# Chunked attention and gated feed-forward in one kernel: transposing transfers for q, k and P from tile 11 instead of tile 15, and batch 2's v loaded earlier

## The chip, the cores and the metric

One Trainium2 chip, one of its cores. The metric is the device time of one execution in microseconds (us): the median of 3 runs is 245.34 (245.0 to 245.46). A profiled execution of the same kernel took 244.74, of which the profile's span, from the first to the last instruction, is 242.7. The granted TensorE clock was 0.998 in it.

## What is computed

```python
# q, k, v: (4 batches, 8 heads, 768, 64); mem_k, mem_v: (4, 8, 8, 64)
for c in range(24):                       # chunks of 32 rows
    q_c = q[:, :, 32*c:32*c+32]
    k_full = [mem_k, k[16 rows left .. 8 rows right of the chunk]]    # v_full alike
    scores = q_c @ k_full.T / 8
    a = exp(scores - max); a = a / sum
    out[:, :, 32*c:32*c+32] = a @ v_full
x = out as 3072 tokens x 512
y = (relu(x @ w_gate) * (x @ w_val)) @ w_out       # 512 -> 1536 -> 512
```

The output is 3072 x 512 in float32.

## The kernel before

The 3072 tokens are 24 **tiles** of 128 rows, six to a batch: tile 11 is the last of batch 1, tiles 12 to 17 are batch 2. Attention works tile by tile, for all 8 heads at once. The feed-forward works on eight **blocks** of 2, 2, 2, 4, 4, 4, 4 and 2 tiles (block 3 is tiles 6 to 9, block 4 is tiles 10 to 13, block 5 is 14 to 17), so that its matmuls are 256 or 512 columns wide.

One tile's attention, in order:

- q and k are loaded by GpSimd's queue (load_qk, L250) into buffers qk_b, rows on partitions. They must be transposed to have the 64 elements of a head on partitions. Up to tile 14 TensorE does it (qk_t, L271: four transposes of 128x128 each for q and for k into PSUM, L275; then ScalarE or VectorE copies them to qT and kT, qk_copy L285). From tile LATE_QK = 15 on a **transposing transfer** does it (qk_transfer, L277, issued by SyncE at L283): q goes straight to qT, k to a buffer k_t (three of them), from which it is copied to kT.
- scores (L297): 32 small matmuls into s_ps, L309. A tile that isn't the last of its batch also needs k of the next tile.
- softmax: row_max and subtract on VectorE (L322, L329), exponent on ScalarE (L337), row_sum, reciprocal, normalise on VectorE (L341, L345, L352) into p_n (three buffers).
- P is transposed too: by TensorE up to tile 14 (p_t, L354: four transposes, L358, and a copy), from LATE_P = 15 on by a transposing transfer (p_transfer, L360, issued at L362) into pT.
- values (L368): 16 matmuls of P with v into xT_ps (L388), and a copy to the block's xT.

For batches 1 to 3, v lies in v_bd, two buffers used in turn: batch 2 has the one that batch 0 used, after it was set to zero (z0, L471 to L474), batch 3 the one of batch 1. A batch's v comes in two big transfers and two small ones (load_v_rows, L185), eight transfers put the memory's rows in (mem_rows, L168), and sixteen copies on ScalarE and VectorE duplicate rows within v_bd ("up", L194, L626).

The feed-forward of a block: 12 pairs of gate and value products (first, L407: g_ps, v_ps, four matmuls each), relu on ScalarE (L413), product on VectorE (gate, L419), then the output products (second, L432: 12 matmuls a tile), a copy and a store. g_ps, v_ps and out_ps share four PSUM banks.

**The order of the work** isn't written out. schedule() (L682) is a planner in Python that runs at build time: each op has engines with a cost, a list deps of ops that must be done (with a lag, if given), resources that it takes and gives, and a priority. The planner walks through a time of its own and hands each op to a free engine; the instructions are emitted in that order, and each engine then runs its own in order. The list deps is read by the planner alone: the semaphores on the chip follow from which tiles an instruction reads and writes, and from a rotation of eight semaphores for transfers of GpSimd's queue and eight for those of SyncE and ScalarE, so that at most eight are in flight. A transposing transfer costs ISSUE = 1.4 of SyncE in the plan and is taken as landed LAND = 4.5 (q, k) or LAND_P = 3.0 (P) later; work on TensorE that belongs to attention is planned a MARGIN of 1.0 after its inputs. GpSimd's transfers are not planned but listed: load() calls in a fixed order (L640 to L675); for batch 2 it is q, k up to k of tile 16 (late[5:21]), then the four of v and the eight memory rows, then q of tile 16 and on (late[21:33]).

Of the kernel before, what the change touches and what calls it, by code (L numbers as in the profile page):

```python
# [19 lines left out]
def kernel(  # L20
# [32 lines left out]
    BAND0 = 48  # L53
    UT = 3

    LATE_QK, LATE_P = 15, 15

    KEY_RUNS = ((0, CH, 0), (KW, 64, CH), (CH, KW, CTX))
    assert sum(BLOCKS) == NT and NMEM == 8 and D == 64 and H == 8
# [391 lines left out]
    def op(key, eng, fn, deps=(), prio=(0,), take=(), give=(), after=()):  # L451
        ops[key] = dict(eng=eng, fn=fn, deps=list(deps), prio=prio, take=list(take), give=list(give),
                        after=list(after))
# [7 lines left out]
    def psum16(n):  # L461
        return {"DVE": (0.07 + 0.52e-3 * n, 0.16 + 0.52e-3 * n), "ACT": psum(n)["ACT"]}
# [49 lines left out]
        return gone[-1:] if blk >= 2 else []  # L512


    ISSUE, LAND, SLACK, LAND_P = 1.4, 4.5, 1.0, 3.0

    def pace_t(a):
        return [("s", a - 6)]

    for a in range(NT):  # L520
        b, t = divmod(a, TPB)
        last = t == TPB - 1
        for i in (1, 0):
            if b == 0:
                if t % 2 == 0:
                    for j in range(2):
                        op(("t", a + j, i), {"PE": 0.3}, lambda e, a=a, i=i, j=j: pair_t(a // 2, i, j),
                           [("pl", a // 2, i), "ib", ("new", b)], (1, a - i, -2 + j), ["aps"])
                        op(("tc", a + j, i), psum16(HP * 128) if t else {("ACT", "DVE")[j]: psum16(HP * 128)[("ACT", "DVE")[j]]}, lambda e, a=a, i=i, j=j: pair_copy(a // 2, i, j, engine[e]),
                           [("t", a + j, i)], (1, a - i, -2 + j), (), ["aps"])  # L530
                continue
            if a >= LATE_QK:
                op(("t", a, i), {"SP": ISSUE}, lambda e, a=a, i=i: qk_transfer(a, i),
                   [(("qk", a, i), SLACK), ("new", b)],
                   (1, a - i, 0), ["kt"] if i else [], [("qk", LAND)], pace_t(a))
                if i:
                    op(("tc", a, i), {"DVE": (0.2, 0.29), "ACT": (0.52, 0.62)}, lambda e, a=a, i=i: qk_copy(a, i, engine[e]),
                       [(("t", a, i), LAND)], (1, a - i, 0), (), ["kt"])
                continue
            op(("t", a, i), {"PE": 0.24}, lambda e, a=a, i=i: qk_t(a, i), [("qk", a, i), "ib", ("new", b)],  # L540
               (1, a - i, 0), ["aps"], ["qk"], pace(max(a - i, 0)))
            op(("tc", a, i), psum16(HP * 128), lambda e, a=a, i=i: qk_copy(a, i, engine[e]), [("t", a, i)],
               (1, a - i, 0), (), ["aps"])
# [38 lines left out]
    for rank, (blk, m) in enumerate(seq):  # L582
        n = BLOCKS[blk]
# [34 lines left out]
    for b in range(1, B):  # L618
        for n in range(2 * HP):
            hp, par = divmod(n, 2)  # L620
            for m in range(TPB // UT):
# [3 lines left out]
                   lambda e, b=b, par=par, i0=i0, i1=i1: upper(b, par, i0, i1, engine[e]),  # L625
# [13 lines left out]
    late = [(a, i) for a in range(TPB, NT) for i in (1, 0)]  # L639
# [22 lines left out]
    for b in range(1, B):  # L662
        deps = ([("z0", hp, c0) for hp in range(HP) for c0 in range(0, NCH, 8)] if b > 1 else [("z1", hp) for hp in range(HP)]) + ([("v", TPB * (b - NSET + 1) - 1)] if b > NSET else [])
        if b == 1:
            for n in range(2 * HP):
                op(("mr", b, n), {"SP": 0.72}, lambda e, n=n: mem_rows(nc.sync, 1, n),
                   deps + [(("vm", 0), 0.2), (("vm", 1), 0.2)], (0,))
        for par in range(2):
            load_v_op(b, par, deps)
        if b > 1:  # L670
            for n in range(2 * HP):
                load(("mr", b, n), 192, 0.22, lambda b=b, n=n: mem_rows(nc.gpsimd, b, n),
                     deps + [(("vm", 0), 0.2), (("vm", 1), 0.2)])
        for a, i in late[5 if b == 1 else 9 + 12 * (b - 1):21 + 12 * (b - 1)]:
            load_qk_op(a, i)  # L675

    WARM = 18.0
# [4 lines left out]
    def schedule():  # L682
        done, started, times = {}, set(), [0.7]
        free = {e: 0.7 for e in ("PE", "ACT", "DVE", "SP", "POOL")}
        queue_end, flying, gives = 0.0, [], [(WARM + 0.15, "fps")]
# [28 lines left out]
        while len(started) < len(ops) + len(loads):  # L714
            t = heapq.heappop(times)
            while times and times[0] <= t + 1e-9:
                heapq.heappop(times)
            for g in [g for g in gives if g[0] <= t + 1e-9]:
                gives.remove(g)
                room[g[1]] += 1  # L720
            flying = [f for f in flying if f > t]
            moved = True
            while moved:
                moved = False
                for e in ("POOL", "PE", "ACT", "DVE", "SP"):
                    if free[e] > t + 1e-9:
                        continue
                    if e == "POOL":
                        if n_load == len(loads):
                            continue  # L730
                        o = loads[n_load]
                        if len(flying) >= 8 or not ready(o, t):
                            continue
                        n_load += 1
                        key = o["key"]
                        if o["n"]:
                            end = t + 0.62 + 0.27e-3 * o["n"]
                            queue_end = max(queue_end, end + 0.8) + o["work"]
                            flying.append(queue_end + 1.0)
                            done[key] = queue_end + (1.2 if n_load < 8 else 4.5 if key[:2] == ("vl", 1) else 2.4 if n_load < 45 else 6.0 if key[0] == "vl" else 4.0)  # L740
                        else:
                            end = done[key] = t + max(o["work"], 0.6)
                        fn = o["fn"]
                    else:
                        o = None
                        soon = False
                        for _, key in todo[e]:
                            late_pe = e == "PE" and t > 36.0 and ops[key]["prio"][0] == 1
                            if ready(ops[key], t, MARGIN if late_pe else 0.0):
                                o = None if soon and key[0] in ("up", "z0") else ops[key]  # L750
                                break
                            soon = soon or ready(ops[key], t + 0.3)
                        if o is None:
                            if e == "PE" and 1.3 < t < WARM:
                                order.append((t, lambda: idle_product(256)))
                                free[e] = t + (0.213 if t < 9.0 else 0.11)
                                heapq.heappush(times, free[e])
                            elif e == "PE" and t <= 1.3:
                                heapq.heappush(times, 1.31)
                            continue  # L760
                        for x in o["eng"]:
                            todo[x].remove((o["prio"], key))
                        d = o["eng"][e]
                        d, lat = d if isinstance(d, tuple) else (d, d)
                        d *= (1.8 if e == "PE" and t < 8.0 and key[0] in ("t", "p", "sh", "f") else 1.0)
                        end = t + d
                        done[key] = end + 0.25 if e == "PE" else t + lat + 0.08

                        if queue_end > t:
                            queue_end += 1.1 if e == "SP" and key[0] in ("t", "pc") else 0.7 if key[0] == "oc" else 0.0  # L770
                        fn = lambda o=o, e=e: o["fn"](e)
                        for g in o["give"]:
                            g, lag = g if isinstance(g, tuple) else (g, 0.0)
                            gives.append((done[key] + lag, g))
                            heapq.heappush(times, done[key] + lag)
                    for r in o["take"]:
                        room[r] -= 1
                    started.add(key)
                    for k in users.get(key, ()):
                        missing[k] -= 1  # L780
                        if not missing[k]:
                            offer(k)
                    order.append((t, fn))
                    free[e] = end
                    for x in (end, done[key], done[key] + 0.2, done[key] + 1.5, done[key] + MARGIN):
                        heapq.heappush(times, x)
                    moved = True
            assert times, [k for k in ops if k not in started][:20]
        return order

    for _, fn in schedule():
        fn()
# [30 lines left out]
```

## Time and profile before

| what | value |
|---|---|
| median of 3 runs | 245.34 us |
| profiled execution | 244.74 us, span 242.7 us |
| TensorE matmul busy | 235.8 us, 97% of the span |
| VectorE, ScalarE, GpSimd busy | 61%, 56%, 32% |
| q, k transposes on TensorE at L275 | 72 |
| P transposes on TensorE at L358 | 60 |
| transposing transfers: k_t, qT, pT | 9, 9, 9 |
| loads of q and of k at L254 | 18 and 18, 128 KB each, 7.0 and 7.2 us from issue to landing in the median |
| first transfer of batch 2's v | issued at 67.46 us |

Times of instructions are counted from the span's start. The page's first part gives busy time for each engine, the second the span in 40 slices of 6.07 us with a digit of busy tenths each; "DMA" there is the mean busy share of the core's 16 DMA engines. "PE" is TensorE's matmuls, "PEld" its weight loads, DVE VectorE, ACT ScalarE, POOL GpSimd, SP SyncE. A matmul's duration in the group rows is its latency; matmuls overlap, so what one costs on a busy TensorE is read from the distance to the next start, or from the chain of work that ended last. For transfers, the trace also has the times at which their semaphores rise, 16 steps for each; "landing" below is the last of these.

### The profile page before, as it was taken

The numbers are of one execution on the slowest core, as the hardware profiler recorded it, in microseconds if no ns is written. First come the engines' busy times: TensorE is split into PE (matmuls) and PEld (weight loads), VectorE is DVE, ScalarE is ACT, GpSimd is POOL, SyncE is SP. The second block draws the span as 40 slices with busy tenths as digits, with TensorE's granted clock in tenths as the row PEclk, the third lists the DMA queues.
The fourth block names the chain that finished last, engine by engine and source line by source line (L and its number), as shares of the span: only waits on it lengthen the run. The fifth ranks groups of instructions, "written<-read, shape, count | busy, mean of one in ns | idle before, by whom it ended". The sixth has DMA issues, their size and how long they took to land.

```text
span 242.7 us, 6546 instructions
## 1 busy us (share of the span) xinstructions
PE 235.8 (97%) x2706; PEld 140.8 (58%) x2706; DVE 147.9 (61%) x296; ACT 136.0 (56%) x288; POOL 77.9 (32%) x102
## 2 busy tenths in 40 slices
PE   7898999999999999999999999999999999999994
PEld 5587887884589545554544545554445444445873
DVE  6674876988877458977549999894431043410430
ACT  7477777767885499665756674453332233312432
POOL 8975689235984396037430000000000000000000
PEclk9999999999999999999999999999999999999999
DMA  6999999999999999999990142651001210012102
GB/s 72 172 179 203 201 164 172 193 131 134 191 195 154 80 168 136 120 124 153 116 218 7 36 53 48 131 133 24 0 0 46 86 43 0 3 43 86 43 3 86
DMA packets 96413, 25.17 MB, mean 104 GB/s; under 512 B 87424, under 2 KB 93312, under 8 KB 96384
## 3 DMA queue, kind: packets, MB, share of 16 engines
q0 software_dynamic: 76128, 14.65, 83.5%
q1 hardware_dynamic: 16656, 3.82, 15.0%
q10 hardware_dynamic: 3600, 6.29, 8.1%
q8 instruction: 21, 0.34, 0.7%
q14 instruction: 8, 0.07, 0.1%
HBM read 28.55 MB, written 6.29 MB: 144 GB/s over the span
## 4 chain that ended last, share of the span: by engine, by line
PE 88%; ACT 4%; DMA 2%; POOL 2%; DVE 2%; issue 1%; ACTq 0%; POOLq 0%
PE v_ps L407 26%; PE g_ps L407 25%; PE out_ps L432 22%; PE xT_ps L388 3%; DMA v_n<-in_v_dram 2%; PE s_ps L309 2%; PE idle_ps L141 2%; PE vs_ps L215 2%; PE xT_ps L381 2%; PE pT_ps L358 2%; ACT v_bd L79 1%; PE qk_ps L275 1%; PE qk_ps L236 1%; POOL qk_p L227 1%; ACT o_sb L79 1%
## 5 line engine op out<-in xcount | busy, mean ns | idle before, releaser
L419 DVE TENSOR_TENSOR gvT<-v_ps,g_relu 128x256 f16<-128x256 f32 (+1 forms) x96 | 52.9, 554 | 58.2 <-PE v_ps L407 43.2
L407 PE MATMUL v_ps<-xT,w_val_sb 128*128 128x256 f16 (+1 forms) x384 | 78.2, 326 | 0.1
L407 PE MATMUL g_ps<-xT,w_gate_sb 128*128 128x256 f16 (+1 forms) x384 | 78.2, 326 | 0.0
L413 ACT ACTIVATE g_relu<-g_ps 128x256 f16<-128x256 f32 (+1 forms) x96 | 47.0, 491 | 47.6 <-PE g_ps L407 45.9
L432 PE MATMUL out_ps<-w_out_sb,gvT 128*128 128x512 f16 (+2 forms) x300 | 65.3, 371 | 0.0
L407 PEld LDWEIGHTS <-w_gate_sb 128*128 128x128 f16 x384 | 36.3, 98 | 23.1
L407 PEld LDWEIGHTS <-w_val_sb 128*128 128x128 f16 x384 | 36.0, 98 | 22.3 <-issue 0.5
L432 PEld LDWEIGHTS <-gvT 128*128 128x128 f16 x300 | 27.9, 98 | 29.9
L79 ACT COPY o_sb<-out_ps 128x512 f32<-128x512 f32 (+2 forms) x25 | 14.2, 567 | 31.8 <-PE out_ps L432 25.6
L337 ACT ACTIVATE p_exp<-dif 128x256 f16<-128x256 f32 (+2 forms) x72 | 19.6, 340 | 4.4 <-DVE dif L329 3.5
L322 DVE TENSOR_REDUCE mx<-s_ps 128x8 f32<-128x512 f32 x24 | 16.5, 688 | 5.6 <-PE s_ps L309 5.4
L341 DVE TENSOR_REDUCE sm<-p_exp 128x8 f32<-128x512 f16 x24 | 16.4, 683 | 4.4 <-ACT p_exp L337 4.1
L254 POOL DMA_DIRECT2D qk_b<-in_q_dram x18 | 16.4, 912 | 7.4 <-DMA v_bd<-in_v_dram 5.5
L254 POOL DMA_DIRECT2D qk_b<-in_k_dram x18 | 16.2, 903 | 5.5 <-DMA w_out_sb<-in_moe_w_out_dram 4.4
L79 ACT COPY v_bd<-v_bd 24x768 f16<-24x768 f16 (+1 forms) x20 | 15.6, 818 | 2.2 <-ACT o_sb L79 1.2
L352 DVE TENSOR_TENSOR p_n<-p_exp,rinv 128x512 f16<-128x512 f16 x24 | 16.5, 687 | 0.4
L329 DVE TENSOR_TENSOR dif<-s_ps,mx 128x512 f32<-128x512 f32 x24 | 16.4, 682 | 0.2
L185 POOL DMA_DIRECT2D v_bd<-in_v_dram x12 | 10.9, 920 | 12.5 <-PE v_ps L407 11.8
L168 POOL DMA_DIRECT2D v_bd<-vmem x16 | 10.5, 661 | 12.5 <-DMA v_bd<-in_v_dram 10.5
L79 ACT CAST xT<-xT_ps 128x512 f16<-128x512 f32 x17 | 9.9, 583 | 6.2 <-PE xT_ps L388 4.8
L141 PE MATMUL idle_ps<-idle 128*128 128x256 bf16 x69 | 11.5, 319 | 1.1 <-DVE warm L475 1.1
L388 PEld LDWEIGHTS <-v_bd 128*128 128x128 f16 x288 | 9.7, 96 | 3.2 <-issue 0.2
(57 smaller groups left out, 179.5 us busy)
## 6 DMA issues: line engine op xcount, KB each, us to landing
out_dram<-o_sb ACTq DMA_DIRECT2D x23, 256.0 KB
qk_b<-in_k_dram POOLq DMA_DIRECT2D x18, 128.0 KB, 7.2
qk_b<-in_q_dram POOLq DMA_DIRECT2D x18, 128.0 KB, 7.0
v_bd<-in_v_dram POOLq DMA_DIRECT2D x6, 384.0 KB, 11.5
w_out_sb<-in_moe_w_out_dram POOLq DMA_DIRECT2D x2, 768.0 KB, 10.5
qk_p<-in_k_dram POOLq DMA_DIRECT2D x3, 256.0 KB, 5.7
qk_p<-in_q_dram POOLq DMA_DIRECT2D x3, 256.0 KB, 6.6
v_n<-in_v_dram POOLq DMA_DIRECT2D x6, 128.0 KB, 6.5
```

The source lines that it names most:

```text
L79: nc.scalar.copy(o, i)
L254: nc.gpsimd.dma_start(qk_b[a, i], bass.AP(tensor=x.tensor, offset=x[b, 0, 128 * t, 0].offset, ap=[[D, 128], [S * D, H], [1, D]]))
L322: nc.vector.reduce_max(SM[a, "mx"], s4, axis=AX.X)
L329: nc.vector.tensor_tensor(out=SM[a, "dif"].rearrange("p (m r) a s -> p r m a s", r=2), in0=S_ps.pop(a).rearrange("p r (m a) s -> p r m a s ...
L337: nc.scalar.activation(p[:, :, :, s0:s0 + k1 - k0], dif[:, :, :, k0:k1], ACT.Exp, scale=SCALE)
L341: nc.vector.reduce_sum(SM[a, "sm"], SM[a, "p"], axis=AX.X)
L352: nc.vector.tensor_tensor(out=P_n[a], in0=SM.pop((a, "p")), in1=rinv_b, op=ALU.mult)
L388: nc.tensor.matmul(ps[:, hp, r], lhsT=v_bd[b % NSET][:, hp, 4 * t + g, :], rhs=x[:, hp, r], start=True, stop=True)
L407: nc.tensor.matmul(ps, lhsT=w[:, f, 128 * m:128 * m + 128], rhs=xTs[blk][:, f, :], start=(f == 0), stop=(f == NFC - 1))
L413: nc.scalar.activation(st["r", m], st.pop((0, m)), ACT.Relu)
L419: nc.vector.tensor_tensor(out=st["gv"][:, m, :], in0=st.pop((1, m)), in1=st.pop(("r", m)), op=ALU.mult)
L432: nc.tensor.matmul(st["o", t, c], lhsT=st["gv"][:, m, 128 * t:128 * t + 128], rhs=w_out_sb[:, m, c[0]:c[1]], start=(m == 0), stop=(m == ND ...
```

## The change

```diff
-    LATE_QK, LATE_P = 15, 15
+    LATE_QK, LATE_P = 11, 11
...
-    ISSUE, LAND, SLACK, LAND_P = 1.4, 4.5, 1.0, 3.0
+    ISSUE, LAND, SLACK, LAND_P = 1.5, 5.0, 1.0, 4.5
...
             if a >= LATE_QK:
                 op(("t", a, i), {"SP": ISSUE}, lambda e, a=a, i=i: qk_transfer(a, i),
-                   [(("qk", a, i), SLACK), ("new", b)],
+                   [(("qk", a, i), SLACK), ("new", b)] + [("vl", 2, n) for n in range(2) if 10 <= a < 15],
                    (1, a - i, 0), ["kt"] if i else [], [("qk", LAND)], pace_t(a))
...
-        for a, i in late[5 if b == 1 else 9 + 12 * (b - 1):21 + 12 * (b - 1)]:
+        for a, i in late[(5, 14, 33)[b - 1]:(14, 33, 36)[b - 1]]:
             load_qk_op(a, i)
...
                         if queue_end > t:
-                            queue_end += 1.1 if e == "SP" and key[0] in ("t", "pc") else 0.7 if key[0] == "oc" else 0.0
+                            queue_end += 1.5 if e == "SP" and key[0] in ("t", "pc") else 0.7 if key[0] == "oc" else 0.0
```

q, k and P of tiles 11 to 14 go by transposing transfers instead of TensorE. In the plan, the q and k transfers of tiles 11 to 14 wait for the two big transfers of batch 2's v ("vl"). In GpSimd's list the four transfers of that v and its eight memory rows stand before k of tile 13 instead of after k of tile 16: seven loads move behind them. The plan takes a transposing transfer as longer (ISSUE, LAND, LAND_P, and 1.5 instead of 1.1 added to its estimate of the busy DMA queue). pace(), which in the plan keeps a tile's transposes on TensorE back until the feed-forward has come to a certain point, then holds for tiles up to 10 instead of 14; a transfer is only placed after the scores of the tile six before it (pace_t).

## Prediction

> **What bounds the kernel now.** First the busy shares, then the span in slices:
>
> ```profile
> PE 235.8 (97%) x2706; PEld 140.8 (58%) x2706; DVE 147.9 (61%) x296; ACT 136.0 (56%) x288; POOL 77.9 (32%) x102
> PE   7898999999999999999999999999999999999994
> DMA  6999999999999999999990142651001210012102
> ```
>
> TensorE is full in every slice but the first four and the last, so time is saved only by taking work from it, and lost where it waits. The DMA engines are full until slice 21 (127 us) and nearly idle later. Next the chain of work that ended last:
>
> ```profile
> 86.69 0.45 PE qk_ps L275 x8
> 87.13 0.86 PE v_ps L407 x4
> ...
> 92.66 0.45 PE qk_ps L275 x8
> ...
> 234.36 4.55 PE out_ps L432 x24
> 238.94 0.49 ACT o_sb L79
> ```
>
> From 80 us on it is TensorE alone, and the transposes stand in it: eight at L275 move the next product by 0.45 us. The timeline of TensorE gives the other steps: 0.86 for four matmuls of 512 columns, 0.65 for three of L432, 0.22 for four P transposes (96.74 to 96.96), about 0.34 for a tile's scores, 0.40 for its values. I added these along the program's order from the start of block 3 (85.66): for the kernel before, the last output products come out at 234.39; the chain has 234.36. So there is no hidden wait in this stretch, and the same sum over the changed order gives due times.
>
> **What the change removes.** By the two programs' orders, TensorE loses 32 transposes at L275 (q, k of four tiles) and 16 at L358. 32 x 0.45/8 = 1.78 us and 16 x 0.22/4 = 0.88 us: **2.66 us** of the chain. Until 85.66 TensorE's order is the same in both. The sum over the changed order ends at 231.73 instead of 234.39 if nothing waits. On VectorE and ScalarE eight copies out of PSUM go (q and P, 0.42 or 0.58 each), and four of k read k_t instead (0.28 or 0.62); those engines are 61% and 56% busy, beside TensorE: I count nothing.
>
> The groups with their shapes show another number:
>
> ```profile
> L358 PE MATMUL pT_ps<-band,p_n 128*128 128x128 f16 x60 | 5.8, 220 | 0.2 <-DVE qT L81 0.2
> L275 PE MATMUL qk_ps<-ident_b,qk_b 128*128 128x128 bf16 x72 | 5.8, 220 | 0.0
> ```
>
> 220 ns is one transpose from its start to its end, but they overlap; only the step of 56 ns is worth anything on a full engine. The Trainium skill, page "TensorE: Matmul & The Clock Gate", Part 4: PE-mode transpose, gives about 275 ns for a transpose in a kernel's context; as an estimate 48 of these would be 13.2 us. No row of the chain agrees.
>
> **What it adds.** Twelve transposing transfers of 128 KB, all in the full stretch. In the plan those of q and k wait for batch 2's v; in the program no semaphore of v stands ahead of them. Each waits for its own load, for its place in the rotation of eight, and k for a free k_t. So k of tile 11 is issued when it has landed, at 63.5, behind nothing on SyncE. The issues before:
>
> ```profile
> 60.81 0.88 POOL L254 DMA_DIRECT2D qk_b<-in_k_dram  x1
> ...
> 67.46 1.33 POOL L185 DMA_DIRECT2D v_bd<-in_v_dram  x1 [0.52 <-DVE p_n L352]
> ```
> ```profile
> 71.98 1.31 SPq L283 DMA_TRANSPOSE k_t<-qk_b  x1
> ...
> 98.82 2.69 SPq L283 DMA_TRANSPOSE qT<-qk_b  x1
> 101.72 1.75 SPq L283 DMA_TRANSPOSE k_t<-qk_b  x1
> 103.56 1.28 SPq L283 DMA_TRANSPOSE qT<-qk_b  x1
> ...
> 136.57 1.19 SPq L362 DMA_TRANSPOSE pT<-p_n  x1
> ```
>
> Before, too, the first (k of tile 15) left as soon as its load was there (71.96). By the landing semaphores, these transfers took 8.6, 8.6, 7.7, 6.3 and 2.4 us; the longest took 11.5 (issued at 73.50, beside v) and 10.4 (91.32), the shortest of the full stretch 4.0 (107.23).
>
> **Step 1, v of batch 2.** Its first transfer leaves at 60.8 instead of 67.46 (the seventh load earlier; v_bd is cleared by 56). Before, both halves had landed 15.3 us after the first issue, at 82.75, with three transposing transfers between; now four lie between: 60.8 + 15.3 + some 1.4 = 77.5 (each such transfer takes at most 242.7 x 15.0% / 27 = 1.35 us of all 16 engines, by the queue row "q1 hardware_dynamic: 16656, 3.82, 15.0%"). This matters as the copies within v_bd now stand earlier on both engines: after 33 relus on ScalarE stands one that waits for the second half, reached at about 78.5. Of TensorE's work only the last product of block 2's first output tile is behind it; adding copy, relu and gate (0.83, 0.42, 0.42), TensorE waits only if v lands after about 81. Cost 0 at 77.5.
>
> **Step 2, q and k of tile 13 on.** These loads now follow v: before, the next load left 1.5 us after v (84.26) and landed after 4.35; so k of tile 13 lands at about 83.5, and with the latencies before (7 to 10 us) k13 is transposed at about 90.5 and k14 at 96.5; scores of tiles 12 and 13 are due at 98.9 and 102.3, and the copies to kT stand on ScalarE at about 98 and 99. Two to seven us spare. k15 must wait for the k_t of tile 12, whose copy stands behind the fourth relu of block 3 (93.7): it lands at about 101.5, and the relu behind its copy can bear 104. Cost 0.
>
> **Step 3, P of tile 11.** The tightest. Scores of tile 11 are due at 92.29; in VectorE's new order normalise stands behind the gate of block 3's sixth pair, which TensorE ends at 97.0; gate, reciprocal and normalise (0.69, 0.12, 0.69) give 98.6, the issue 98.7. SyncE is free by then: q of tile 15 left at about 95. Values of tile 11 are due at 106.07: **7.4 us** for the transfer, where TensorE's transpose and copy needed less than 2. Bounds from rows: 2.4 (alone, at 136.57) and 10.4 or 11.5 (deepest queue), so a wait of 0 to 3.0 or 4.1. I take 8.1, the middle of 8.6, 7.7 and 6.3 leaned to the later rows' upper end, since loads are still running (19 behind v instead of 12) and two or three transposing transfers are outstanding: **0.7 us** of waiting. Behind it in TensorE's order stands everything, so this is lost; but the deadlines that follow move along.
>
> **Step 4, the next ones.** k16 and q16, k17, q17 queue behind P of tile 11 on SyncE, 1.3 us apart. By the same sums P12 has 8.4 us, P13 7.7 and P14 about 7, and k16 some 9 before its copy holds back relus and scores. The 0.7 waited in step 3 is added to each of P12's and P13's, whose softmax comes before the wait or beside it. From 107 the third batch's v is in the queue; beside it transfers took 7.0 (108.79) and 6.5 (115.85), what P14 has. So 0 more, with 2 as the other end (10.4 at P13). After 127 transfers take 2.4 to 4 and have 7: nothing.
>
> **Sum.** -2.66 + 0.7 = -1.96. Profiled 244.74 - 1.96 = 242.8 (span 240.7); the median of the runs stands 0.6 above the profiled execution: 245.34 - 1.96 = **243.4**.
>
> **Rivals.** *All hidden*: the transfers take 7.4 or less at step 3, as at 103.56 (6.3): 242.7. For it: the 7.4 us given; TensorE's order leaves more to the rest. The Trainium skill, "Advanced Engine Details and Errata", X-Bar Transpose, says that on trn2 transposing DMAs are as fast as regular ones. The page's regular loads of 128 KB take 7.0 and 7.2 in the median here, which would lead to this case; the rows of 8.6 speak against it, that of 2.4 is from an idle stretch.
>
> *P arrives late* (the other side): values wait for pT. Each us over 7.4 costs one; from 10.1 the gain is gone. At the 10.4 of 91.32, with the 0.5 us more for tile 12 or 13, whose softmax doesn't move with the wait: 245.34 - 2.66 + 3.0 + 0.5 = 246.2. For it: the deepest queue, twelve more transfers in a full stretch. Against: only one row of the 98 to 107 stretch is that long, when five were outstanding.
>
> *The hold isn't one*: k11 to q12 run beside v as said, and v comes no earlier than before, 82.75. Then ScalarE's copy blocks relu and gate: 82.75 - 81 = 1.7 us, 244.4 with step 3 in its place. Against: 15.3 us from issue held with other transfers between.
>
> *Transposes cost their duration*: 48 x 0.22 = 10.6 off, 234.8. The steps in the chain deny it.
>
> **How the numbers follow.** Forecast 0.5 (243.4, own range 242.9 to 244.3), all hidden 0.25, P late 0.15, no earlier v 0.09, full duration 0.01. A change of 0.2% (0.5 us) is about what a measurement tells from none. Faster takes nearly all of the first two (0.73), half of the case without an earlier v, and the last: 0.78. The rest of that case and the nearest part of P late give 0.10 within; the remainder, 0.12, is slower. The range goes from 242.4, the full 2.66 with 0.3 for the rows' rounding and the runs' spread, to 245.4, which takes in half of P late; outside stay the rest of it, the last rival and little else, under 0.2.
>
> **What would show it.** After: 40 and 44 transposes at L275 and L358; the last output products at 231.7 plus the waits; idle time of TensorE before L388 "<-DMA pT<-p_n", about 0.7 in total; k_t issued at 63.5, ahead of v's landing at 77.5; no wait before L407 or L432 at 78 to 86. Wrong it would be if TensorE waits before L309 for qT or kT, if a gate or relu stands behind a v_bd or kT copy for over 1 us, or if transfers of P take over 10 us at 98.

## The result and the profile after

The changed kernel takes **257.74 us** (median of 6, 255.09 to 262.63), the kernel before 244.80 in the same batch: a ratio of 1.0474 (1.0408 to 1.054). 243.4 was predicted: by the medians it lost 12.9 us instead of gaining 2.0. The ratio is of the four shorter of the six runs; the other two, both at 262, are left out of it, and as the profiled execution (262.63, span 260.9) is one of these, kinds and places of the waits are read from it and differences from the runs' times.

First part and slices of the profile after, as shown of before:

```profile
PE 239.1 (92%) x2658; PEld 139.5 (53%) x2658; DVE 147.8 (57%) x291; ACT 135.3 (52%) x285; POOL 77.6 (30%) x102
PE   7998999999989899759993699999999999999994
PEclk9999999999999999977998899999999999999999
DMA  7999999999998999999999991151001320002102
```

A slice is 6.52 us here. TensorE is no longer full in several of the slices 12 to 23 (72 to 150 us), its granted clock dips in 18, 19, 22 and 23, and the DMA engines are nearly full until slice 24 (157 us) instead of 21 (127 us). TensorE's waits, from its timeline (start, time, engine, line, operation; in brackets the idle time before and what ended it):

```profile
78.72 0.60 PE L407 MATMUL g_ps<-xT,w_gate_sb 128*128 128x256 f16 x4 [1.74 <-ACT g_relu L413]
...
86.46 2.98 PE L432 MATMUL out_ps<-w_out_sb,gvT 128*128 128x512 f16 x13 [1.09 <-DVE gvT L419]
...
107.55 0.30 PE L309 MATMUL s_ps<-kT,qT 64*32 64x64 bf16 x26 [1.41 <-ACT kT L79]
...
112.25 1.02 PE L407 MATMUL g_ps<-xT,w_gate_sb 128*128 128x512 f16 x4 [1.71 <-ACT g_relu L413]
115.13 0.59 PE L388 MATMUL xT_ps<-pT,v_bd 128*128 128x32 f16 x16 [1.86 <-DMA pT<-p_n]
...
142.25 0.59 PE L388 MATMUL xT_ps<-pT,v_bd 128*128 128x32 f16 x16 [4.54 <-DMA pT<-p_n]
...
148.98 0.55 PE L388 MATMUL xT_ps<-pT,v_bd 128*128 128x32 f16 x16 [2.40 <-DMA pT<-p_n]
```

The first two stand behind ScalarE's copies within v_bd: one starts at 77.43, when the first half of batch 2's v has landed (77.41), one at 84.70, when the second has (84.68). The third and the fourth (a relu that stands behind a copy on ScalarE) wait for k of tiles 14 and 15, which landed at 106.86 and 111.07; the last three are values waiting for P. From the chain of work that ended last:

```profile
63.86 20.82 DMA v_bd<-in_v_dram
...
85.56 0.39 ACT g_relu L413
...
85.97 0.44 DVE gvT L419
...
86.46 2.98 PE out_ps L432 x13
...
103.66 11.43 DMA pT<-p_n
115.09 0.04 issue
115.13 0.59 PE xT_ps L388 x16
...
125.11 7.95 DMA pT<-p_n
133.06 0.05 issue
133.32 15.62 DMA pT<-p_n
148.94 0.04 issue
148.98 0.55 PE xT_ps L388 x16
```

Before, this chain was TensorE alone from 80 us on; now a transfer of 20.82, one of 11.43 and one of 15.62 stand in it. With one more wait of 0.20 before L388 the waits add to 14.95. Span against span the loss is 260.9 - 242.7 = 18.2; with 2.66 saved, 5.9 are left beyond the waits. Most of that is the clock after the waits. The windows of 2 us (length, TensorE's busy time, then PEld, DVE, ACT, POOL, the granted clock, DMA share, GB/s):

```profile
112.00:114.00 2.00, 1.02 (x4) 0.39 (x4) 1.76 (x3) 0.69 (x2) 0.87 (x1) 1.00 2.72 152
114.00:116.00 2.00, 0.87 (x49) 0.74 (x48) 1.68 (x4) 1.54 (x5) 0.00 (x0) 0.58 1.46 80
116.00:118.00 2.00, 2.00 (x17) 0.73 (x6) 0.81 (x3) 0.96 (x2) 1.45 (x2) 0.50 1.68 153
118.00:120.00 2.00, 2.00 (x6) 0.76 (x5) 1.88 (x3) 0.31 (x1) 0.37 (x1) 0.50 1.67 157
120.00:122.00 2.00, 2.00 (x39) 0.67 (x36) 0.60 (x1) 0.98 (x4) 1.63 (x2) 0.71 1.85 154
...
140.00:142.00 2.00, 0.00 (x0) 0.00 (x0) 0.61 (x1) 0.00 (x0) 0.00 (x0) 0.91 1.45 65
142.00:144.00 2.00, 1.75 (x20) 0.92 (x20) 0.00 (x0) 1.12 (x4) 0.00 (x0) 0.50 1.31 119
144.00:146.00 2.00, 2.00 (x9) 0.77 (x8) 1.34 (x3) 0.41 (x3) 0.00 (x0) 0.74 1.59 111
```

The clock is 0.50 behind the waits at 112 to 115 and behind that of 4.54; products of 512 columns that step by 0.86 elsewhere step by 1.70 to 1.82 there. What is missing from a clock of 1.00 in these windows adds up to 5.1 us (2 us times each shortfall), the most that it can have cost; some of it fell on idle time. So the clock is most of the 5.9 and not all; the rest is not traced. The Trainium skill, "TensorE: Matmul & The Clock Gate", Why this matters for your kernels, warns of gaps over about 3 us between bursts of matmuls; the trace agrees for the wait of 4.54, while the first halving stands behind two shorter waits, 1.71 and 1.86, with 1.0 us of work between.

The queues, from GpSimd's and SyncE's timelines:

```profile
62.05 3.67 POOL L185 DMA_DIRECT2D v_bd<-in_v_dram  x4
```
```profile
64.50 1.31 SPq L283 DMA_TRANSPOSE k_t<-qk_b  x1
65.92 1.57 SPq L283 DMA_TRANSPOSE qT<-qk_b  x1
67.58 2.50 SPq L283 DMA_TRANSPOSE k_t<-qk_b  x1
70.27 1.21 SPq L283 DMA_TRANSPOSE qT<-qk_b  x1
```

So v did leave earlier, and the four transfers the plan had placed behind its landing left while it was in flight. By the landing semaphores that v came at 84.68 (77.5 was predicted, 82.75 it was before), the four took 9.3 to 15.6 us, and batch 3's v, issued at 116.55 instead of 107.01, took 30.0 us instead of 11.5, beside transposing transfers of 7.1 to 15.6. A late v also holds up the loads behind it, which GpSimd issues in their listed order:

```profile
77.69 0.63 POOL L168 DMA_DIRECT2D v_bd<-vmem  x1 [8.50 <-DMA v_bd<-in_v_dram]
...
84.96 1.26 POOL L168 DMA_DIRECT2D v_bd<-vmem  x2 [5.32 <-DMA v_bd<-in_v_dram]
86.21 1.06 POOL L254 DMA_DIRECT2D qk_b<-in_k_dram  x1
```

It stood idle for 8.50 and 5.32 us until v's halves had landed, so k of tile 13, the load at 86.21, left late.

### The profile page after: what moved, and what is told of

Read it like the earlier page. It is cut to its first block, busy times and chain, and to the rows that moved or that the text cites. A ratio compares the mean times of both kernels' runs of the same rounds, so it can differ in the third digit from the quotient of the medians.

```text
span 260.9 us, 6458 instructions
## 1 busy us (share of the span) xinstructions
PE 239.1 (92%) x2658; PEld 139.5 (53%) x2658; DVE 147.8 (57%) x291; ACT 135.3 (52%) x285; POOL 77.6 (30%) x102
## 4 chain that ended last, share of the span: by engine, by line
PE 63%; DMA 30%; issue 2%; ACT 2%; POOL 1%; DVE 0%; SPq 0%; ACTq 0%; POOLq 0%
PE v_ps L407 19%; PE g_ps L407 18%; PE out_ps L432 16%; DMA v_bd<-in_v_dram 15%; DMA pT<-p_n 13%; PE idle_ps L141 2%; PE xT_ps L388 2%; PE s_ps L309 1%; PE qk_ps L236 1%; DMA kmem_f<-in_mem_k_dram 1%; PE xT_ps L381 1%; POOL v_bd L185 1%; PE vs_ps L215 1%; ACT kT L79 1%; POOL qk_b L254 1%
## 5 line engine op out<-in xcount | busy, mean ns | idle before, releaser
L407 PE MATMUL g_ps<-xT,w_gate_sb 128*128 128x256 f16 (+1 forms) x384 | 79.4, 330 | 3.4 <-ACT g_relu L413 3.4
L407 PE MATMUL v_ps<-xT,w_val_sb 128*128 128x256 f16 (+1 forms) x384 | 80.8, 334 | 0.1
L407 PEld LDWEIGHTS <-w_val_sb 128*128 128x128 f16 x384 | 36.7, 99 | 24.7 <-issue 2.7
L79 ACT COPY o_sb<-out_ps 128x512 f32<-128x512 f32 (+2 forms) x25 | 14.2, 567 | 34.9 <-PE out_ps L432 28.8
L79 ACT COPY v_bd<-v_bd 24x768 f16<-24x768 f16 (+1 forms) x22 | 17.7, 818 | 6.3 <-DMA v_bd<-in_v_dram 5.1
L254 POOL DMA_DIRECT2D qk_b<-in_k_dram x18 | 16.3, 903 | 13.5 <-DMA qk_b<-in_k_dram 4.6
L388 PE MATMUL xT_ps<-pT,v_bd 128*128 128x32 f16 x288 | 9.8, 178 | 9.0 <-DMA pT<-p_n 9.0
L388 PEld LDWEIGHTS <-v_bd 128*128 128x128 f16 x288 | 9.5, 97 | 12.4 <-issue 9.5
L79 ACT CAST xT<-xT_ps 128x512 f16<-128x512 f32 x16 | 9.3, 584 | 11.5 <-PE xT_ps L388 10.2
L141 PE MATMUL idle_ps<-idle 128*128 128x256 bf16 x69 | 11.8, 325 | 1.1 <-DVE warm L475 1.1
## 6 DMA issues: line engine op xcount, KB each, us to landing
w_out_sb<-in_moe_w_out_dram POOLq DMA_DIRECT2D x2, 768.0 KB, 11.2
```

What stands on the lines that cost most here:

```text
L79: nc.scalar.copy(o, i)
L141: nc.tensor.matmul(TMP["idle"][:, 0:N], lhsT=idle[:, 0:128], rhs=idle[:, 0:N], start=True, stop=True)
L254: nc.gpsimd.dma_start(qk_b[a, i], bass.AP(tensor=x.tensor, offset=x[b, 0, 128 * t, 0].offset, ap=[[D, 128], [S * D, H], [1, D]]))
L388: nc.tensor.matmul(ps[:, hp, r], lhsT=v_bd[b % NSET][:, hp, 4 * t + g, :], rhs=x[:, hp, r], start=True, stop=True)
L407: nc.tensor.matmul(ps, lhsT=w[:, f, 128 * m:128 * m + 128], rhs=xTs[blk][:, f, :], start=(f == 0), stop=(f == NFC - 1))
```

## The experiments

Ratios are to the kernel before, in the same batch. Landing times are those of the last of a transfer's 16 steps.

**One part of the change alone.** The constants are the edit:

```diff
-    LATE_QK, LATE_P = 11, 11
+    LATE_QK, LATE_P = 11, 15     # e2_qk11
+    LATE_QK, LATE_P = 15, 11     # e3_p11
+    LATE_QK, LATE_P = 15, 15     # e4_order
```

> P by TensorE up to tile 14, q and k by transfer from 11. Beside-v theory: v of batch 2 still lands at 83 or later and the waits before 87 us stay, those for P go: 249 to 252. Load theory: 8 of the 12 transfers are still there, so two thirds of the loss: about 252.

> q and k by TensorE up to tile 14, P by transfer from 11. Beside-v theory: nothing stands beside batch 2's v, which lands at about 75; P of tiles 13 to 15 meets batch 3's v and TensorE waits 4 to 7 us for it: 247 to 251. Load theory: 4 of 12 transfers, a third of the loss: about 248, with waits for P of tile 11 as well.

> No transfer more than before (15, 15), but v of batch 2 ahead of tiles 13 on, and the changed costs in the plan. Both theories: 244 to 246, since no transfer is added; above 247 the order of the loads itself costs something that neither names.

Measured: q and k alone 257.68 (1.0492, 1.0417 to 1.0568); P alone 250.49 (1.0224, 1.0184 to 1.0264); load order and plan alone 244.54 (0.9991, 0.9977 to 1.0006). The new load order costs nothing; q and k cost as much as the whole change, where both theories expected 252 at most; P by itself costs about half. With q and k alone, in a profiled execution of 256.46, batch 2's v lands at 83.06: late as in the changed kernel. With P alone no transposing transfer lies beside that v, which lands at 75.19; its waits come after 100, the longest (2.66) at 137.5 for a transfer of P that took 11.4 us. With the order alone v lands at 73.48.

**A hold that is one.** Two small transfers that read the landed v, ahead of the first q, k transfer on SyncE, make it wait for v on the chip:

```diff
+        if (a, i) == (11, 1):
+            for par in range(2):
+                nc.sync.dma_start(kmem_f[0:1, par, 0:D // 2].bitcast(F16),
+                                  v_bd[0][D * par:D * par + 1, 0, 0, D * par:D * par + D])
```

> Beside-v theory (a transposing transfer in flight beside a batch's v slows both far below the rate of either): with q, k of tiles 11 and 12 truly waiting for v of batch 2, that v lands at about 75 us instead of 84.7, the waits before 87 us in TensorE go, and the time falls from 255 to 257 to 248 to 251; the waits beside batch 3's v stay. Load theory (twelve more transfers in a window whose DMA engines are full, wherever they stand): the same work only comes later, the time stays at 254 or rises.

Measured: 250.35 (1.0208, 1.0159 to 1.0258). V lands at 74.52, and no wait of TensorE over 0.3 us is left between 60 and 113. Over half of the loss (7 of 12.9 us) was v meeting transfers that were to be held; the rest comes later, around batch 3's v, which took 23.6 us (11.5 in the kernel before).

**Is it the form of v's transfer?** A kernel of stages alone, and two cuts of v's big transfers to one row in 32 (as shown in the changed kernel, and with b > 2 on top of the hold):

```diff
-        load(("vl", b, par), CH * n, CH * n * 1.03e-3, lambda: load_v_rows(b, par, 0, CH, 0, n), (), (), deps)
+        load(("vl", b, par), CH * n, CH * n * 1.03e-3, lambda: load_v_rows(b, par, 0, 1 if b > 1 else CH, 0, n), (), (), deps)
```

> Leaves out the whole computation: the outputs are zeros. It runs stages one after the other, each started on SyncE, GpSimd and ScalarE together once all transfers of the stage before have landed: 1 and 4 transposing transfers alone; the two big transfers of a batch's v alone (32 partitions each, 6144 pieces of 64 elements together); six loads of q and k alone (128 partitions, 6144 pieces of the same size); the v pair beside 1, 2, 4 and 8 transposing transfers; the six loads beside 1, 2, 4 and 8; the v pair beside two stores; each of the two beside 4 transfers and two stores; and the 4-transfer stages again. Theory 1 (the form of v's transfer and transposing transfers slow one another): the v pair takes about 13 us alone (as with nothing beside it in the run with a real hold: 61.29 to 74.52), four transfers some 2.4 + 3 x 1.3 = 6.5 us alone, and together over 20 us, with transfers of 9 us and more; the six loads with four transfers stay within 4 us of the six loads alone. Theory 2 (any load is slowed alike by transposing transfers, v has only more pieces): the v pair and the six loads, which have the same pieces, take the same time beside the same number of transfers, both over 18 us beside four. Theory 3 (the engines simply add up the work): every mixed stage takes the sum of its parts at most, 13 + 4 x 1.3 = 18 us for the v pair with four, in both forms.

> The changed kernel, but the big transfers of v of batches 2 and 3 bring one row in 32 (the other rows of these batches keep old values): order, waits, plan and all other transfers stay. Theory 1 (v beside transposing transfers is what costs): no wait of over 0.5 us behind v, k_t, qT or pT is left, transposing transfers take 5 to 9 us, and the time is what TensorE's work gives: 244.5 - 2.66 = 241.9, at most 243. Theory 2 (twelve more transposing transfers are too many for SyncE's queue in a full stretch, with or without v): waits for pT stay, and the time is 247 or more.

> The changed kernel with the real hold (transfers from tile 11 on wait until batch 2's v has landed, 250.35), and the big transfers of batch 3's v bring one row in 32 (the others keep old values). Theory 1: what is left of the loss, 250.35 - 241.9 = 8.4 us, comes from batch 3's v beside the denser transfers: the time falls to 242 to 243.5, with no wait for pT of over 0.5 us after 113. Theory 2 (the number of transfers): 248 to 250, the waits for pT at 118 to 133 stay.

Measured in the stages, from the first issue to the last landing: four transposing transfers alone 6.4 us, the v pair (v's two big transfers) alone 8.7, six loads alone 8.5; with four transfers 11.9 and 13.0 for the stage of the v pair, 11.8 for that of the loads. Theories 1 and 2 fall, both of which expected over 18 or 20: v's form is nothing special, and each transfer adds 0.8 to 1.1. In the kernel, v cut gives 248.51 (1.0159, 1.0138 to 1.018), and the hold with batch 3's v cut 249.09 (1.0204, 1.0167 to 1.0241); theory 1 misses both, and the figures are those of theory 2 there (the number of transfers). Cutting v takes away 9 of 12.9 us, but of what the hold leaves (5.8) cutting batch 3's v takes away only 1.3, so v isn't all of it. What is left in the first, from the waits:

```profile
PE xT_ps L388 <- DMA pT<-p_n: 5.2, 1, 5.2
```

One wait, for a transfer of P that took 11.2 us from 114.85 beside the memory rows, three transfers of its kind, stores and loads.

**The memory rows.** Their stages, and in the kernel their eight transfers cut to one chunk of 24:

```diff
+        c = NCH if b == 1 else 1
...
-            v_bd[b % NSET][p, hp, :, D * par:D * par + D],
+            v_bd[b % NSET][p, hp, 0:c, D * par:D * par + D],
             bass.AP(tensor=src.tensor, offset=src.offset,
-                    ap=[src.ap[0], [0, NCH], [1, D]]))
+                    ap=[src.ap[0], [0, c], [1, D]]))
```

> Leaves out the whole computation: the outputs are zeros. Stages as before, each started on all queues together once the stage before has landed, now with the eight transfers of a batch's memory rows (8 partitions each, read and written in SBUF) and with TensorE, ScalarE and VectorE at work beside. Measured so far, by the stages of the first such kernel: v pair alone 8.7 us, four transposing transfers alone 6.4, the v pair with four 11.9 and 12.95, six loads with four 11.8: some 0.8 to 1.1 per transfer, v and the loads alike, so the form of v's transfer isn't what slows both in the kernel. Theory 4 (the memory rows are what does it: their few long pieces hold the engines up, and the transposing transfers with them): the rows alone take 6 us or more, and the v pair with four transfers and the rows 18 us or more, transfers 9 us and more. Theory 5 (compute engines at work on SBUF slow the transfers): the v pair with four transfers beside work takes 15 us or more without rows. Theory 3 (all of it adds up): rows add under 3 us to any stage, work adds under 1.

> The changed kernel, but the eight transfers of memory rows of batches 2 and 3 bring one chunk's rows instead of 24 (the others keep old values); v, order, waits and plan stay. Theory 4 (memory rows beside transposing transfers): batch 2's v lands by 77 instead of 84.7, batch 3's within 15 us, and the time is 243 to 250. Theories 3 and 5: 255 to 258, as the changed kernel.

> The changed kernel, with both cuts: the big transfers of v of batches 2 and 3 bring one row in 32, and their memory rows one chunk's. With v cut alone 248.5 was measured, and one wait of 5.2 us was left, for pT of a transfer that took 11.2 us from 114.85, beside memory rows, three transfers of its kind, stores and loads. Theory 4: that wait goes, transfers take at most 8 us, and the time is 242 to 243.5. Theory 3 and 5: 247 to 249, with the same wait.

Measured: rows alone 6.9 us; v pair with four transfers 11.9, with the rows as well 15.9; compute engines at work beside add at most 2.3. That lies between the theories: the rows make the stage of v with transposing transfers 4.0 us longer, that of v without them 2.6. V's own landing, counted from its first issue, moves less: from 11.2 to 13.1 us with transposing transfers beside, and not at all without (8.7). In the kernel: rows cut 249.54 (1.0191, 1.0163 to 1.022), both cut **243.08** (0.9935, 0.9913 to 0.9957). With the rows cut the time is inside what theory 4 expected, but not its signs: in the profile (252.36) batch 2's v still landed at 80.61 and batch 3's took 26.2 us. Each cut alone leaves about 4 to 5 us of loss, both leave none. In the profile of the kernel with both, with all twelve new transfers in it, TensorE is full from 84 to 236 us (before first, then this kernel):

```profile
84.00:236.00 152.00, 151.86 (x1418) 78.14 (x1417) 86.03 (x163) 76.17 (x156) 22.68 (x28) 1.00 0.64 73
```
```profile
84.00:236.00 152.00, 152.00 (x1383) 76.50 (x1382) 83.53 (x156) 71.89 (x150) 12.91 (x20) 1.00 0.52 72
```

From block 3's first product to the last output products it needs 232.76 - 86.86 = 145.90, the kernel before 234.36 - 85.66 = 148.70: 2.80 less, for 2.66 predicted. Of this 1.4 us reach the time, since block 3 starts 1.2 us later than before in that execution (86.86 for 85.66); why is open.

**Is it the transposing?** The twelve new transfers (a < 15; P alike) as plain copies of the same bytes, in pieces of 256 bytes. With them ran q and k alone with the real hold, and the cut rows on top of the hold in two forms; in the second, which also ran with the rows whole, the plan places the transfers nearer to their scores:

```diff
-        nc.sync.dma_start(o, qk_b.pop((a, i)).rearrange("p h d -> p (h d)"), transpose=True)
+        nc.sync.dma_start(o, qk_b.pop((a, i)).rearrange("p (x h) d -> p x (h d)", h=2))
...
-        return [("s", a - 6)]
+        return [("s", a - 3)]
```

> The changed kernel, but the twelve new transfers (q, k and P of tiles 11 to 14) copy their tile as it is, in pieces of 256 bytes, instead of transposing it, so that the scores and values of these tiles are of untransposed data; order, waits, plan, sizes and the transfers of the later tiles stay. If what slows batch 2's v is that the transfers beside it transpose: that v lands by 78 instead of 84.7, the new transfers take under 6 us, and the time is 243 to 250 (batch 3's v still meets the later ones). If any transfer of this size on that queue does it (the sum of bytes): v lands at 82 or later and the time is 255 to 258.

> The real hold, with q and k by transfer from tile 11 but P only from tile 15 (TensorE's saving is 1.78 us of 2.66). Without the hold this was 257.7. If too many transfers beside batch 2's and batch 3's v with their memory rows are the cause: no transfer beside batch 2's v and four fewer before batch 3's, so 243 to 247. If the number of transfers after 105 stays the trouble, as in the kernel with the hold and P from tile 11 (250.35): 248 to 251.

> The real hold, and in the plan the q and k transfers of a tile are placed after the scores of the tile three before it instead of six, so that fewer of them stand beside batch 3's v. Nothing is left out. Theory 1: fewer transfers beside that v, which lands in 12 to 18 us instead of 21.8, P's transfers take 6 to 9 us beside it, and the time is 243 to 247. Theory 2 (number of transfers in all): as the real hold alone, 249 to 251.

> The real hold (250.35), and the memory rows' transfers of batches 2 and 3 bring one chunk's rows instead of 24 (the others keep old values); both v's whole. If rows and v beside transposing transfers each take their share: batch 3's v lands within 16 us of its issue instead of 23.6, and the time is 244 to 247. If v alone is enough: 249 to 251.

> The real hold with the q and k transfers placed after the scores of the tile three before theirs (249.99; one wait of 4.55 us at 126.9, for a transfer of q that took 15.5 us beside batch 3's v and its memory rows), and these rows cut as in the run beside it. If the rows are needed for it: that transfer takes under 10 us, the wait goes, and the time is 242 to 245, at or below the kernel before. If not: 248 to 251.

Measured: plain copies 250.40 (1.0248, 1.0204 to 1.0292). The transfers of a window of 60 to 90 us (KB each, median us to landing of v's two big ones), in the order kernel alone (none beside), with copies, and in the changed kernel:

```profile
v_bd<-in_v_dram POOLq DMA_DIRECT2D x2, 384.0 KB, 9.0
```
```profile
v_bd<-in_v_dram POOLq DMA_DIRECT2D x2, 384.0 KB, 13.3
```
```profile
v_bd<-in_v_dram POOLq DMA_DIRECT2D x2, 384.0 KB, 18.1
```

From v's first issue to its last landing these are 11.8, 15.1 and 22.6 us: four copies cost 3.3, four transposing transfers 10.8, or 2.7 each. With copies v lands at 77.22, as expected for the case that transposing is what slows it; the four copies took 6.4 to 9.5 us, over the 6 expected, and the time is just over its range. A loss of 5.7 us is left there, with one wait of 7.53 for P of tile 14: its copy, issued at 113.29 among transposing transfers beside batch 3's v, took 15.3 us.

The others: real hold, q and k from 11, P from 15: 255.29 (1.0423, 1.0398 to 1.0448), a miss by 8 us. Its q, k transfers keep SyncE's queue full up to batch 3's v, which takes 27.8 us, and P comes behind both:

```profile
PE xT_ps L392 <- DMA pT<-p_n: 9.3, 1, 9.3
```

The hold with transfers placed later: 249.99 (1.0209, 1.0184 to 1.0235), no better. With the rows cut: the hold 248.65 (1.0144, 1.01 to 1.0188), the second form 247.15 (1.0106, 1.0067 to 1.0145). The rows are a share here too, but both runs missed what was expected of them: a loss of 2 to 4 us is left beside batch 3's v without whole rows. I read this as the number of transfers in SyncE's queue there; no run shows it by itself.

**Only between the two v's.** New transfers for tiles 11 and 12, or 11 to 13, alone; tiles 13 and 14, or 14, back on TensorE; the real hold:

```diff
-    LATE_QK, LATE_P = 11, 11
+    LATE_QK, LATE_P = 15, 15
+    EARLY = (11, 12)             # e9_two; (11, 12, 13): e10_three
...
-            if a >= LATE_QK:
+            if a >= LATE_QK or a in EARLY:
```

> Nothing is left out. The real hold, with transposing transfers for q, k and P of tiles 11 and 12 only, then TensorE for 13 and 14 as before, transfers again from 15: TensorE loses 16 transposes at L275 and 8 at L358, 0.89 + 0.44 = 1.33 us. If the loss comes only where transposing transfers lie beside a v with its memory rows: the new ones lie between the two v's (75 to 106), those beside batch 3's v are those of the kernel before, 5 or 6, and the time is 244.7 - 1.3 = 243.4, up to 244.2 with a small wait. If any further transfer in the full stretch costs: 245 to 248.

> The same with tiles 11, 12 and 13 (P of 13 is due just when batch 3's v is loaded): TensorE loses 2.0 us. If the loss comes only beside a v: one or two more transfers come to lie beside batch 3's v, so a wait for pT of tile 13 of 1 to 3 us, 244 to 246. If any further transfer in the full stretch costs: 247 to 250.

Measured, in 5 rounds: two tiles 244.56 (0.9992, 0.9964 to 1.002), with runs from 243.45 to 250.11; three tiles **243.84** (0.9964, 0.9947 to 0.998), from 243.09 to 244.92. Two tiles are no faster than before, a little over what was expected (243.4 to 244.2); three tiles beat the kernel before by 0.9 us, which is little, but the interval does not include 1. In the profile of the second batch 2's v lands at 73.51 and batch 3's in 14.2 us, and from 84 on TensorE has no gap:

```profile
84.00:236.00 152.00, 151.98 (x1391) 76.53 (x1390) 82.22 (x154) 74.54 (x154) 19.32 (x24) 1.00 0.71 82
```

From block 3's first product to the last output products it needs 233.16 - 86.32 = 146.84, 1.86 less than before, where 2.0 was removed. So further transfers in the full stretch cost next to nothing there in the three-tile form, where most of them lie between the v's; its expected wait for P of tile 13 didn't come. Why the two-tile form spreads over 6 us is open.

**The queue as it stands at batch 2's v.** Loads, v, rows, stores and compute together, with nothing, four transposing transfers, or four copies:

> Leaves out the whole computation: the outputs are zeros. Stages as in the first two such kernels. First four transposing transfers alone, then four plain copies of the same size in pieces of 256 bytes alone; each of the two beside the v pair; each beside six loads; and twice over the queue as it stands at batch 2's v: four loads, the v pair and the eight memory rows behind them, three stores, the compute engines at work, with no further transfers, with four transposing ones that each wait for their own load, and with four plain copies that do. If transposing is what is dear beside v, as in the kernel (84.7 against 77.2): in the last form the v pair lands at least 5 us later with transposing transfers than with copies, and copies cost under 1 us each everywhere. If the kernel's other work is needed for that: transposing transfers cost 0.8 to 1.1 us each in the last form too, as in the stages before, so at most 3 us more than copies.

Measured, v's first issue to its last landing, two stages each: nothing 10.6 and 9.5; transposing 16.3 and 14.2; copies 11.6 and 11.1. The windows of the first stage of each kind (median us to landing):

```profile
v_bd<-in_v_dram POOLq DMA_DIRECT2D x2, 384.0 KB, 12.4
v_bd<-vmem POOLq DMA_DIRECT2D x8, 24.0 KB, 13.4
k_t<-qk_b SPq DMA_TRANSPOSE x4, 9.5
```
```profile
v_bd<-in_v_dram POOLq DMA_DIRECT2D x2, 384.0 KB, 8.8
k_t<-qk_b SPq DMA_DIRECT2D x4, 128.0 KB, 6.6
v_bd<-vmem POOLq DMA_DIRECT2D x8, 24.0 KB, 8.7
```

A transposing transfer costs v 1.3 us here and a copy 0.3, from the means (5.2 / 4 and 1.3 / 4). With transposing transfers v lands 4.7 and 3.1 us later than with copies: between the two theories (5 or more, 3 or less), in the direction of the kernel's 2.7 and 0.8 each, at half their size or less. What makes it twice as dear in the kernel stays open. One trace of it, in the changed kernel: of the 16 landing steps of v's first half, 15 had come by 69.5 and the last came at 77.4; in the order kernel, without transfers beside, the last came 0.8 behind (68.9, 69.7). Which engine lags, and on what, the trace doesn't name.

## Why the prediction was wrong

- **What is removed: right.** The rows after have the predicted counts, and the saving is there where nothing hides it (2.80 for 2.66).

```profile
L358 PE MATMUL pT_ps<-band,p_n 128*128 128x128 f16 x44 | 4.3, 220 | 0.3 <-DVE qT L81 0.3
L275 PE MATMUL qk_ps<-ident_b,qk_b 128*128 128x128 bf16 x40 | 3.2, 220 | 0.0
```

- **Issue order: right.** The hold is no wait on the chip; k of tile 11 left at 64.50 (63.5), ahead of v's landing.
- **Step 1, v at 77.5: wrong, and the first thing to fail.** The term was "some 1.4" for a fourth transfer beside v, from a queue row's share of busy time, with a base of 15.3 from another backlog. Measured from the case with none beside (11.8), four transposing transfers add 10.8, or 2.7 each where the busy share gave 1.35: the share counts the time of the transfer's own packets, not what it holds up. That copies landed at 77.22, close to the 77.5, is chance, as the base of 15.3 held three transposing transfers. The waits were 1.74 and 1.09. The first stood behind v's first half (77.41), which no term had; with TensorE that much later, the threshold of "about 81" for the second half moves to about 83, and 84.68 cost 1.09.
- **Step 2, cost 0: wrong.** The rule for the next load held (86.21, 1.5 us after v), so most of the lateness is that of v: k of tile 13 was transposed at 98.84 and not at 90.5, k of tile 14 at 106.86 and not at 96.5, for which the scores waited 1.41 at 107.55, and k of tile 15 at 111.07 and not at 101.5, for which relu and product waited 1.71 at 112.25. The transfers took 8.9 to 12.2 us, where 7 to 10 was assumed.
- **Step 3, 8.1 us for P of tile 11: the size was wrong.** It was issued at 103.66 (98.7) and took 11.43; the wait was 1.86. The bound of 11.5 covers it, but that row stood beside v, and this transfer didn't: outstanding were four transposing transfers and eight loads that took 14 to 18 us. The row of 10.4 (issued at 91.32, before the stretch that the prediction names) and those issued at 93.85 and 97.46 (9.3 each), which it doesn't list, were nearer than the middle taken.
- **Step 4, "0 more": wrong, and the largest.** It took transfers beside batch 3's v from the kernel before (7.0 and 6.5), where 3 were issued in that v's time. Here 14 were, which I put to all before being late and P's coming on top: the first seven took 7.1 to 8.4 us, the next four, from 129.28 on, 12.9 to 15.6, and the last three 7.3 to 11.1, with waits of 0.20 + 4.54 + 2.40 for P and the halved clock behind the 4.54.
- **The rivals.** "The hold isn't one" named the mechanism and got its 0.09; its price, 1.7, stopped at the first wait. "P arrives late" was priced at a latency of 10.4 once. Neither saw that a late v delays the next transfers into the next v. The Trainium skill's sentence that a transposing transfer is as fast as another ("Advanced Engine Details and Errata", X-Bar Transpose) stood behind a rival at 242.7; the runs decide against it. Alone, four take 6.4 us and four copies 3.9 (17.18 to 23.62, 24.54 to 28.45); most of that is the issue, 1.3 us apart instead of 0.6, since one takes 2.5 us to its landing and a copy 2.0. Beside v they cost four times a copy in the stage and three in the kernel.

Shown by runs: the load order is free; the missing hold is over half of the loss; the new transfers cost nothing once both v's big transfers and the memory rows are cut, and either cut alone takes away 8 to 9 of the 12.9 us; at batch 2's v it is the transposing and not the bytes. Shown by the trace: a late v holds GpSimd, and so the loads behind it. Argued only: why so many transfers come to lie beside batch 3's v, and the split of what is lost there between v, rows and the number of transfers.

## What to carry to other kernels

A dependency that only a planner knows is no wait: look in the emitted order for what really stands ahead of each transfer. Price a transposing transfer by what it does to the transfers beside it, at the place where the most of them meet, and not by its latency alone or its share of busy time. If a big load with a deadline shares the engines, try new transposing transfers in the gap between two such loads, and leave the rest on TensorE; here that form alone gained (0.9 us).

## What the runs showed of the hardware that was not expected

- Four transposing transfers of 128 KB beside a load of 768 KB cost it 5.2 us, four copies of the same bytes 1.3 (stages with loads, rows, stores and compute).
- Eight transfers that spread rows of memory over 8 partitions each, 192 KB in all, take 6.9 us alone; they make a stage with the v pair 2.6 us longer, and one with the v pair and four transposing transfers 4.0.
- Around the landing of batch 2's v the DMA engines stand mostly idle, in the changed kernel with some ten transfers outstanding. There the rate falls from 135 GB/s at 78 us to 4 at 84.75, and the engines' mean busy share from nine tenths to none (the views: slices of 0.75 us from 60). In the order kernel, with no transposing transfer beside v, it falls too, for some 3 us from 73.5, down to 8 GB/s. So the fall by itself is no sign of the transposing: in both, GpSimd waits for v's second half before it issues its next transfers (5.32 and 2.51 us). What keeps that half out until 84.68 is not shown.

```profile
DMA  9999999999999999999999999938952310233699
GB/s 177 144 194 198 210 225 205 148 164 153 158 139 136 92 160 163 167 154 154 127 131 121 75 133 135 98 11 64 77 28 9 26 13 4 16 22 29 43 124 66
```
```profile
DMA  9999999999999999962044999999999999999999
GB/s 173 199 221 164 234 226 166 169 156 152 152 158 158 168 247 231 187 172 65 8 26 33 61 121 103 135 141 170 141 130 138 147 127 125 145 158 165 246 170 166
```
